# Talking-heads attention with two MLPs: half of the score sends on GpSimd's queue, two more places for copies, one query load per head pair

## Chip, cores and metric

The kernel runs on one core of a Trainium2 chip. The metric is the device time of one execution in microseconds (us), as the median of several runs. A profile belongs to one further execution, which has its own time.

## The reference

There are 4 batches, 12 heads, 448 rows and a head width of 64; all values are float32. The attention mixes the heads before and after the softmax, and two MLPs follow on 1792 tokens of width 768.

```python
scores = scale * np.matmul(q, k.transpose(0, 1, 3, 2))
scores = np.einsum('bhij,hg->bgij', scores, w_pre)        # mix of heads
attn = np.exp(scores - np.max(scores, axis=-1, keepdims=True))
attn = attn / (np.sum(attn, axis=-1, keepdims=True) + 1e-09)
attn = np.einsum('bhij,hg->bgij', attn, w_post)           # second mix
x = np.matmul(attn, v)                                    # (b, h, i, d) -> tokens x 768
...
h = x @ w_in                                              # 768 -> 2048
x = (h * np.cos(h)) @ w_out                               # 2048 -> 768
h = np.maximum(np.maximum(x @ w1, x @ w2), x @ w3)        # 768 -> 768
return h @ w_out2
```

## The kernel before, in words

**Score blocks.** Each batch's 448 rows are cut into four blocks of 10, 12, 12 and 11 "slots" of 10 rows (`SBLK`; the last overlaps the third by two rows), 16 blocks in all. Two blocks make a half of a batch. For each block and pair of heads, `qk` multiplies queries by keys on TensorE into two PSUM banks, one for each head; `evac` copies each bank to an SBUF tile s (on VectorE or ScalarE); `send` is a DMA that carries that copy to a grid tile t. The partitions of s are rows; those of t are (row within slot, head) after 4 spare partitions (`PAD`), so that the mix of heads is a matmul over partitions. There are two grids, used in turn; the 4 spare partitions of each are cleared once by `fill`, a DMA from a tile of zeros on ACT's queue.

**Visits.** A block is worked off in visits of two slots. `mix1` (L700) mixes heads from t into PSUM and needs all twelve sends of its block; `rowmax` on VectorE and `soft` on ScalarE make the exponentials e; `guard`, `recip` and `wscale` on VectorE make the divided weights w2s; `mix2` (L741) mixes the exponentials; `keep` copies the result to a2. After the two blocks of a half, `av` (L770) multiplies by the values, `keepx` copies and `out` writes to xT in DRAM. Then come the MLPs, whose first layer's weights and tokens are read and converted while the last blocks are at work.

**Loads and queues.** `qget` (queries), `kget` (keys), `vget` (values), `send`, `out` and the weights' loads are all issued on SP's queue, in one order; ACT's queue carries the first batch's keys, the small weights and `fill`. In DRAM each head's queries stand twice, one copy after the other, so that either head of a pair can be read into either half of the partitions. `qget` is two loads of 64 partitions. GpSimd issues no DMA. Each engine and queue works in the order in which its instructions were written.

**The order.** Class `Plan` deals it when the program is built. Every step has a rank, engines with a cost in us each, steps that it comes after, and places that it takes from a ring of buffers (`BUFS`: s has 6) and frees. The planner goes on in its own reckoned time; of the steps that could start on an engine it takes the one of lowest rank, and where a step may go to several engines, the one that would end first. Steps with `turn=True` are written in the order in which they were added. A copy takes a place of s, and its `send` gives it back, when it has landed.

Of the kernel before, what the change touches and what calls it, by code (L numbers as in the profile page):

```python
# [21 lines left out]
RI = 10  # L22
# [561 lines left out]
def attention(ctx, tc, q, k, v, w_pre, w_post, same_row, xT, tp, mlps):  # L584
# [12 lines left out]
    q = q.rearrange("(b c g d e i) -> b c g d e i", b=B, c=H // 2, g=2, d=2, e=D)  # L597
# [9 lines left out]
    zero = const.tile([PAD, S], F32, name="zero")  # L607
# [3 lines left out]
    for x in (zero, wraw, blk, w1):  # L611
        nc.vector.memset(x, 0.0)
# [5 lines left out]
    score = [(b, i0, RI * slots, slots) for b in range(B) for i0, slots in SBLK]  # L618
# [6 lines left out]
    def fill(n, _):  # L625
        nc.scalar.dma_start(grids[n][:PAD], zero.unsqueeze(1).to_broadcast([PAD, RT, S]))
# [47 lines left out]
    def qk(n, hp, _):  # L674
        b, i0, m, _ = score[n]
# [68 lines left out]
    def half_of(n):  # L744

        n = n // 2 * 2
        return score[n][1], score[n + 1][1] + score[n + 1][2] - score[n][1]

    def keep(v, y, eng):
        n, t, _ = visits[v]  # L750
        half = n // 2
        if ("a2", half) not in live:
            live["a2", half] = ap_.tile([128, JB, H, NHALF], F32, name="a2")
        o = (n % 2) * score[n - 1][2] + RI * (t + y)
        copy(eng, live["a2", half][:, :, :, o:o + RI].rearrange("p j g i -> p (j g) i"),
             live["a", v, y][:].rearrange("p j g a r -> p (j g) (a r)"))
# [5 lines left out]
    def av(n, x, _):  # L762
        m, a2 = score[n - 1][2] + score[n][2], live["a2", n // 2]
        for hp in pairs(x):
            vt = live["v", score[n][0], hp]
# [7 lines left out]
    def keepx(n, hp, eng):  # L773

        xs = live["xs", hp] = xp.tile([128, NHALF], F32, name="xs")
        ps = live["av", hp]
        c = 0
        for x in (n - 1, n):
            _, i0, m, slots = score[x]
            o = i0 - half_of(n)[0]  # L780
            copy(eng, xs[:, o:o + m].rearrange("p (r t) -> p r t", t=slots),
                 ps[:, c:c + m].rearrange("p (t r) -> p r t", r=RI))
            c += m

    def out(n, hp, eng):
        b, (i0, m) = score[n][0], half_of(n)
        queue_of[eng].dma_start(xT[hp * 128:(hp + 1) * 128, b * S + i0:b * S + i0 + m], live["xs", hp][:, :m])
# [10 lines left out]
    HP, per = H // 2, len(SBLK)  # L798
# [4 lines left out]
    for n in range(2):  # L803
        add(fill, (n,), -45.0 + 5.0 * n, {"A": 0.9}, lands=6.0)
    add(wmix, (0,), -39.0, {"V": 0.8}, [("wget", 0), ("wget", 2)])
    add(wmix, (1,), -39.0, {"V": 0.2}, [("wget", 1), ("wget", 2)])
    for n in range(NS):
        b = score[n][0]
        start, end = n % per == 0, n % per == per - 1
        for hp in range(HP):  # L810
            r = (first[n - 1] + 0.5 + 1.5 * hp) if n else -40.0 + hp
            if start:
                early = 8.0 if b else 20.0
                add(qget, (b, hp), r - early, {"D": 1.17}, turn=True, takes=["q"], lands=3.0)
                add(kget, (b, hp), r - early, {"D": 0.5} if b else {"A": 0.6}, turn=True, takes=["k"], lands=3.0)
# [3 lines left out]
            for h in range(2 * hp, 2 * hp + 2):  # L819
                add(evac, (n, h), r, {"A": 0.55, "V": 0.62}, [("qk", n, hp)], turn=True, takes=["s"], frees=[(ring, ("qk", n, hp), h % 2)])  # L820
                if h == 0:
                    plan.add(("new_t", n), r, lambda _: None, {}, [("evac", n, 0)], takes=["t"])
                add(send, (n, h), r, {"D": 0.83}, [("evac", n, h), ("new_t", n)], turn=True, frees=[("s", ("evac", n, h))], lands=3.0)


    for y, (n, t, slots) in enumerate(visits):
# [12 lines left out]
        for c in slots:  # L839
            begin = n % 2 == t == c == 0  # L840
# [4 lines left out]
    for n in range(1, NS, 2):  # L845
        b = score[n][0]
        last = (first + [N])[n + 1] - 1
        ends = [("keep", y, a) for y, x in enumerate(visits) if x[0] in (n - 1, n) for a in x[2]]
        start = ends[0]
        for x in range(HP // 2):  # L850
            r = last + 2.5 + 3.0 * x
            for hp in pairs(x) if n // 2 % 2 == 0 else ():
                add(vget, (b, hp), r - 10.0, {"D": 0.88}, turn=True, takes=["v"], lands=3.0)
            add(av, (n, x), r, {"T": 3.25}, [("vget", b, hp) for hp in pairs(x)] + ends, turn=True, takes=["ps_t"] * 2,
                frees=[("a2", start)] + [("v", ("vget", b, hp)) for hp in pairs(x) if n // 2 % 2])
            for hp in pairs(x):
                add(keepx, (n, hp), r, {"A": 0.45, "V": 0.5}, [("av", n, x)], turn=True, takes=["xs"], frees=[("ps_t", ("av", n, x), hp % 2)])
                add(out, (n, hp), r, {"D": 0.45}, [("keepx", n, hp)], turn=True, frees=[("xs", ("keepx", n, hp))], lands=3.0)
# [144 lines left out]
    for n in range(2):  # L1003
        r = (r0, N - 1)[n] + RANK[("fx", "x1")[n]]
        add(xget, (n,), r, {"D": 3.9}, [("out", 1, hp) for hp in range(H // 2)] + [("out", 3, hp) for hp in range(H // 2)] + [("xget", 0)] * n
# [38 lines left out]
    plan.add(("open_late",), N, open_late, {}, [("keepx", NS - 1, hp) for hp in range(HP)], behind=att_keys)  # L1044
# [70 lines left out]
    halves = 0  # L1115
    for i, (name, (eng, _, needs)) in enumerate(unit.items()):
        kind, x = name
        tags = ["wf"] if kind == "get" and x != "S3" else []
        if kind == "high":
            tags = ["w"] * (halves % 2 == 0)  # L1120
            halves += 1
# [52 lines left out]
```

## Time and profile before

| | |
|---|---|
| median of 3 runs | 1209.25 us (1206.21 to 1214.73) |
| the profiled execution | 1209.98 us |
| its span, first to last instruction | 1208.2 us |
| mean granted TensorE clock | 0.98 of full |
| TensorE (PE) busy | 1150.8 us, 95% |
| VectorE (DVE) busy | 929.1 us, 77% |
| ScalarE (ACT) busy | 637.9 us, 53% |
| GpSimd (POOL) busy | 190.3 us, 16% |
| sends, t<-s on SP's queue | 192 |

Busy shares are means over stages with different limits: the attention part lasts to some 405 us, the MLPs from there to the end. The program names its tiles in the rows: t<-s is a send, mps<-t,w the first mix, aps<-w2s,e the second, ps<-k,q (and aps or mps<-k,q for the first block) the scores, aps<-a,v the product with the values. A "q" behind an engine's name (SPq, ACTq) means what its sequencer issues, DMAs above all. "Before" is the idle time in front of an instruction and what ended it, as far as the profile can tell; where several things were waited for, it is the one that came last by the records.

### The profile page before, as it was taken

The numbers are of one execution on the slowest core, as the hardware profiler recorded it, in microseconds if no ns is written. First come the engines' busy times: TensorE is split into PE (matmuls) and PEld (weight loads), VectorE is DVE, ScalarE is ACT, GpSimd is POOL, SyncE is SP. The second block draws the span as 40 slices with busy tenths as digits, with TensorE's granted clock in tenths as the row PEclk, the third lists the DMA queues.
The fourth block names the chain that finished last, engine by engine and source line by source line (L and its number), as shares of the span: only waits on it lengthen the run. The fifth ranks groups of instructions, "written<-read, shape, count | busy, mean of one in ns | idle before, by whom it ended". The sixth has DMA issues, their size and how long they took to land.

```text
span 1208.2 us, 29520 instructions
## 1 busy us (share of the span) xinstructions
PE 1150.8 (95%) x11886; PEld 938.8 (78%) x11886; DVE 929.1 (77%) x1913; ACT 637.9 (53%) x1436; POOL 190.3 (16%) x172
## 2 busy tenths in 40 slices
PE   4879999999999889999999999999999999999998
PEld 1445655656556779999999999999998989889997
DVE  2666786788789699999999999996865548865445
ACT  1555665566568577565555555555644444344520
POOL 0000000000003120000000000001065455476340
PEclk8889999999999989999999999999999999999999
DMA  6765565654555536444444344430012221322112
GB/s 152 203 186 153 172 177 166 189 177 131 165 153 181 193 99 171 132 128 131 125 131 129 114 131 113 130 111 27 1 53 66 66 66 54 130 71 81 33 59 92
DMA packets 85384, 146.19 MB, mean 121 GB/s; under 512 B 9664, under 2 KB 68224, under 8 KB 85248
## 3 DMA queue, kind: packets, MB, share of 16 engines
q1 hardware_dynamic: 83680, 142.75, 39.8%
q10 hardware_dynamic: 1568, 1.57, 0.6%
q8 instruction: 93, 1.52, 0.5%
q14 instruction: 43, 0.35, 0.1%
HBM read 84.96 MB, written 20.45 MB: 87 GB/s over the span
## 4 chain that ended last, share of the span: by engine, by line
PE 80%; DMA 7%; DVE 6%; issue 3%; POOL 2%; ACT 1%; SPq 0%; DVEq 0%; POOLq 0%; ACTq 0%
PE ps L165 19%; PE ps L167 19%; PE ps L166 19%; PE mps L700 6%; PE aps L770 6%; PE aps L741 6%; PE ps L681 5%; DMA t<-s 3%; DVE nm L708 2%; DMA wf<-w 2%; POOL w L309 1%; DVE wf L298 1%; DMA q<-in_q_dram 1%; DVE a L600 1%; DMA wraw<-in_w_in_dram 1%
## 5 line engine op out<-in xcount | busy, mean ns | idle before, releaser
L165 PE MATMUL ps<-x,w 128*128 128x448 f32 x708 | 262.0, 370 | 6.9 <-ACT x L152 5.1
L167 PE MATMUL ps<-x,w 128*128 128x448 f32 x708 | 259.9, 368 | 1.9 <-DVE x L156 1.3
L166 PE MATMUL ps<-x,w 128*128 128x448 f32 x708 | 260.3, 368 | 0.0
L309 POOL TENSOR_TENSOR w<-wf,w 128x384 fp32r<-128x384 f32 x126 | 142.6, 1154 | 546.7 <-DVE wt L264 370.4
L165 PE MATMUL ps<-gh,w 128*128 128x448 f32 x528 | 193.8, 367 | 0.0
L166 PE MATMUL ps<-gh,w 128*128 128x448 f32 x528 | 193.5, 366 | 0.0
L167 PE MATMUL ps<-gl,w 128*128 128x448 f32 x528 | 193.3, 366 | 0.0
L714 ACT ACTIVATE e<-mps,nm 128x448 f32<-128x448 f32 (+1 forms) x184 | 117.2, 639 | 89.5 <-DVE nm L708 59.6
L165 PEld LDWEIGHTS ps<-x,w 128*128 128x128 f32 x708 | 133.5, 189 | 23.9 <-ACT x L152 5.7
L741 PEld LDWEIGHTS aps<-w2s,e 60*64 60x64 f32 x5760 | 109.1, 136 | 50.3 <-issue 22.6
L167 PEld LDWEIGHTS ps<-x,w 128*128 128x128 f32 x708 | 133.4, 188 | 15.0 <-DVE x L156 2.4
L166 PEld LDWEIGHTS ps<-x,w 128*128 128x128 f32 x708 | 133.6, 189 | 11.2 <-POOL w L132 0.2
L708 DVE TENSOR_REDUCE nm<-mps 128x1 f32<-128x448 f32 (+1 forms) x184 | 110.5, 615 | 32.1 <-PE mps L700 30.7
L700 PE MATMUL mps<-t,w 64*64 64x448 f32 (+1 forms) x720 | 108.8, 573 | 17.7 <-DMA t<-s 10.8
L741 PE MATMUL aps<-w2s,e 60*64 60x60 f32 x5760 | 113.6, 221 | 7.0 <-DVE w2s L728 3.5
L681 PE MATMUL ps<-k,q 64*64 64x448 f32 (+3 forms) x736 | 102.2, 573 | 17.3 <-ACT s L600 11.8
L298 DVE TENSOR_TENSOR wf<-wf 128x384 f32<-128x384 f32 x72 | 57.8, 815 | 71.7 <-POOL w L309 43.8
L306 ACT CAST w<-wf 128x384 fp32r<-128x384 f32 x126 | 60.6, 512 | 90.8 <-DVE wf L298 40.6
L167 PEld LDWEIGHTS ps<-gl,w 128*128 128x128 f32 x528 | 99.1, 188 | 9.0
L165 PEld LDWEIGHTS ps<-gh,w 128*128 128x128 f32 x528 | 99.1, 188 | 8.8
L166 PEld LDWEIGHTS ps<-gh,w 128*128 128x128 f32 x528 | 99.1, 188 | 8.6
L947 DVE TENSOR_TENSOR acc<-ps,acc 128x448 f32<-128x448 f32 x168 | 100.3, 613 | 3.1 <-PE ps L167 3.1
(99 smaller groups left out, 1638.6 us busy)
## 6 DMA issues: line engine op xcount, KB each, us to landing
t<-s SPq DMA_DIRECT2D x96, 210.0 KB
wf<-w SPq DMA_DIRECT2D x96, 192.0 KB
wraw<-in_w_out_dram SPq DMA_DIRECT2D x44, 384.0 KB
wraw<-in_w_dram SPq DMA_DIRECT2D x36, 384.0 KB
wraw<-in_w_in_dram SPq DMA_DIRECT2D x32, 384.0 KB
t<-s SPq DMA_DIRECT2D x48, 192.5 KB
w<-wf SPq DMA_DIRECT2D x48, 192.0 KB
t<-s SPq DMA_DIRECT2D x48, 175.0 KB
```

Source lines behind the costliest of these rows:

```text
L165: mm(w[0], x[0], start=first, stop=False)
L166: mm(w[1], x[0], start=False, stop=False)
L167: mm(w[0], x[1], start=False, stop=last)
L298: eng(raw[x], raw[l], raw[r])
L309: return nc.gpsimd.tensor_sub(A[x][1], w(), f32(A[x][0]))
L681: nc.tensor.matmul(live["s", n, 2 * hp + g][r:end], live["q", b, hp][half, i0 + r:i0 + end], live["k", b, hp][half], start=True, stop=True)
L700: nc.tensor.matmul(live["m", v, a][64 * y:64 * y + 64], w1[k], grids[n % 2][k, t + y, :], start=True, stop=True)
L708: nc.vector.tensor_reduce(nm, of(v, live["m", v, a]), axis=AX.X, op=ALU.max, negate=True)
L714: nc.scalar.activation(of(v, e), of(v, live["m", v, a]), AF.Exp, bias=live["nm", v, a], scale=1.0, accum_out=live["z", v][:, a:a + 1])
L741: nc.tensor.matmul(live["a", v, y][64 * c:64 * c + 64, j, :, a, :], live["e", v, a][k, o:o + 64], live["w2s", v][k, a], start=True, stop=True)
L770: nc.tensor.matmul(ps[64 * g:64 * g + 64, :m], vt[:, j, g, :], a2[:, j, 2 * hp + g, :m], start=j == 0, stop=j == JB - 1)
L947: return nc.vector.tensor_add(acc, po, acc) if fg else nc.scalar.copy(acc, po)
```

## The change

Sends of odd heads go to GpSimd's queue, those of even heads stay on SP's. `fill` becomes a memset on GpSimd of the 4 spare partitions of each grid; the tile of zeros goes. s has 8 places instead of 6, and in the very first block the copies of heads 1, 3, 5, 7 and 9 take the five places of e instead. `qget` becomes one load of 128 partitions: the second copy of a pair's first head and the first copy of its second head, which stand side by side in DRAM. The planner's costs and ranks follow. The table of blocks is written in another way (`HALVES`), with the functions that read it.

```diff
-SBLK = [(0, 10), (100, 12), (220, 12), (338, 11)]
+HALVES = [[[10, 12], [12, 11]]] * B
-BUFS = {"k": 10, "q": 9, "s": 6, "e": 5, "w2s": 3, "v": 7, "xs": 6, "a2": 2, "ps_m": 3, "ps_t": 3, "ps_x": 2}
+BUFS = {"k": 10, "q": 9, "s": 8, "e": 5, "w2s": 3, "v": 7, "xs": 6, "a2": 2, "ps_m": 3, "ps_t": 3, "ps_x": 2}
...
-    q = q.rearrange("(b c g d e i) -> b c g d e i", b=B, c=H // 2, g=2, d=2, e=D)
+    q = q.rearrange("(b c e i) -> b c e i", b=B, c=H // 2, e=4 * D)
...
-    zero = const.tile([PAD, S], F32, name="zero")
...
+    for b, sizes in enumerate(HALVES):
+        i = 0
+        for n, half in enumerate(sizes):
+            start, column = i, 0
+            for slots in half:
+                i = min(i, S - RI * slots)
+                score.append((b, i, RI * slots, slots, 2 * b + n, column))
+                column += RI * slots
+                i += RI * slots
+            halves.append((b, start, i - start, column, range(len(score) - len(half), len(score))))
...
     def fill(n, _):
-        nc.scalar.dma_start(grids[n][:PAD], zero.unsqueeze(1).to_broadcast([PAD, RT, S]))
+        nc.gpsimd.memset(grids[n][:PAD], 0.0)
...
-        for g in range(2):
-            queue_of[eng].dma_start(live["q", b, hp][64 * g:64 * g + 64], q[b, hp, g, 0])
+        queue_of[eng].dma_start(live["q", b, hp], q[b, hp, D:3 * D])
...
+    def copy_place(n, h):
+        return ("e", ep) if n == 0 and h in range(1, 2 * BUFS["e"], 2) else ("s", sp)
+
     def evac(n, h, eng):
         m, ps = score[n][2], live["s", n, h]
-        s = live["s", n, h] = sp.tile([128, S], F32, name="s")
+        place, pool = copy_place(n, h)
+        s = live["s", n, h] = pool.tile([128, S], F32, name=place)
         copy(eng, s[:m], ps[:m])
 
-    def send(n, h, _):
+    def send(n, h, eng):
         slots = score[n][3]
-        nc.sync.dma_start(grids[n % 2][PAD + h:PAD + RI * H:H, :slots, :], live.pop(("s", n, h))[:RI * slots])
+        queue_of[eng].dma_start(grids[n % 2][PAD + h:PAD + RI * H:H, :slots, :], live.pop(("s", n, h))[:RI * slots])
...
-        add(fill, (n,), -45.0 + 5.0 * n, {"A": 0.9}, lands=6.0)
+        add(fill, (n,), -60.0, {"P": 5.0})
...
-            r = (first[n - 1] + 0.5 + 1.5 * hp) if n else -40.0 + hp
+            r = (first[n - 1] + 0.5 + 0.125 * score[n - 1][3] * hp) if n else -40.0 + hp
...
-                add(qget, (b, hp), r - early, {"D": 1.17}, turn=True, takes=["q"], lands=3.0)
+                add(qget, (b, hp), r - early, {"D": 0.57}, turn=True, takes=["q"], lands=3.0)
...
-                add(send, (n, h), r, {"D": 0.83}, [("evac", n, h), ("new_t", n)], turn=True, frees=[("s", ("evac", n, h))], lands=3.0)
+                add(send, (n, h), r, ({"D": 0.83}, {"P": 0.55})[h % 2], [("evac", n, h), ("new_t", n)], turn=True, frees=[(place, ("evac", n, h))], lands=3.0)
...
-                add(out, (n, hp), r, {"D": 0.45}, [("keepx", n, hp)], turn=True, frees=[("xs", ("keepx", n, hp))], lands=3.0)
+                add(out, (half, hp), r, {"D": 0.5}, [("keepx", half, hp)], turn=True, frees=[("xs", ("keepx", half, hp))], lands=3.0)
```

## Rows read from the trace of the kernel before

**Rows 1.** Windows: start:end, length, busy us (instructions) by engine, clock, DMA share, GB/s.

```profile
core 0: us, PE busy (x) PEld busy (x) DVE busy (x) ACT busy (x) POOL busy (x), PEclk, DMA share, GB/s
0.00:30.00 30.00, 13.06 (x57) 3.50 (x58) 8.28 (x22) 4.99 (x9) 0.20 (x4) 0.82 0.61 151
30.00:60.00 30.00, 24.47 (x456) 12.14 (x454) 18.02 (x46) 15.07 (x40) 0.00 (x0) 0.84 0.71 204
60.00:90.00 30.00, 23.02 (x571) 13.52 (x566) 18.88 (x51) 16.23 (x43) 0.00 (x0) 0.83 0.70 186
90.00:120.00 30.00, 28.11 (x631) 17.52 (x631) 19.73 (x56) 14.97 (x45) 0.00 (x0) 0.94 0.53 153
120.00:180.00 60.00, 57.08 (x1412) 35.68 (x1404) 48.55 (x126) 37.18 (x103) 0.00 (x0) 1.00 0.58 173
...
480.00:540.00 60.00, 60.00 (x296) 55.34 (x295) 58.86 (x121) 34.56 (x67) 0.00 (x0) 1.00 0.44 127
```

**Rows 2.** The page: granted TensorE clock in 40 slices of the span, in tenths.

```profile
PEclk8889999999999989999999999999999999999999
```

**Rows 3.** Timeline of the opening: start us, us, engine, line, operation, tiles, [idle before].

```profile
0.73 12.49 SPq L660 DMA_DIRECT2D q<-in_q_dram  x12
...
7.87 1.15 DVE L600 COPY s<-ps 100x448 f32<-100x448 f32 x2 [2.63 <-PE ps L681]
...
13.34 18.74 SPq L691 DMA_DIRECT2D t<-s  x14
...
13.37 1.46 ACTq L626 DMA_DIRECT2D t<-zero  x2
...
14.69 1.69 PE L681 MATMUL mps<-k,q 64*64 64x448 f32 x8
...
23.18 1.28 ACT L600 ACT_TABLE_LOAD   x1 [23.18 <-DMA t<-s]
...
32.45 0.62 DVE L600 COPY s<-ps 120x448 f32<-120x448 f32 x1 [16.53 <-DMA t<-s]
...
34.53 1.84 PE L700 MATMUL mps<-t,w 64*64 64x448 f32 x8
```

**Rows 4.** Chain that ended last, 0 to 130 us: start us, us, what.

```profile
13.34 9.75 DMA t<-s
...
25.11 3.91 DMA t<-s
...
67.15 8.19 DMA t<-s
...
75.41 3.14 DMA t<-s
```

**Rows 5.** Timeline at the changes to blocks 1 and 2.

```profile
49.39 1.65 SPq L691 DMA_DIRECT2D t<-s  x2
...
53.71 1.77 PE L700 MATMUL mps<-t,w 64*64 64x448 f32 x8 [3.06 <-DMA q<-in_q_dram]
...
78.68 1.77 PE L700 MATMUL mps<-t,w 64*64 64x448 f32 x8 [6.13 <-DMA t<-s]
```

**Rows 6.** TensorE's waits, 125 to 200 and 200 to 360: sum us, times, longest.

```profile
PE mps L700 <- DMA t<-s: 3.4, 2, 2.2
...
PE mps L700 <- DMA t<-s: 1.3, 1, 1.3
```

**Rows 7.** Windows of almost only sends, and of loads alone; columns as above.

```profile
24.00:33.00 9.00, 4.84 (x17) 1.16 (x17) 0.55 (x1) 5.19 (x10) 0.00 (x0) 0.50 0.58 187
1.00:10.00 9.00, 4.84 (x16) 1.14 (x16) 5.32 (x14) 0.00 (x0) 0.00 (x0) 1.00 0.97 234
```

**Rows 8.** Views of single tiles and lines: ns min/median/max, first and last start us.

```profile
L691 SPq DMA_DIRECT2D t<-s x192: 755/756/3322, 13.3 to 358.4; - x192
...
L660 SPq DMA_DIRECT2D q<-in_q_dram x48: 465/546/1312, 0.7 to 266.9; - x48
...
L615 DVE MEMSET v<- x7: 485/485/485, 1.5 to 4.8; 128x512 f32 x7
...
L132 POOL TENSOR_TENSOR w<-wf,w x30: 999/1022/1402, 369.9 to 1169.5; 128x384 fp32r<-128x384 f32 x30
```

**Rows 9.** Groups by line: busy us, mean ns, idle before.

```profile
L728 DVE TENSOR_TENSOR w2s<-w2t,rz 128x120 f32<-128x120 f32 (+1 forms) x92 | 26.4, 287 | 0.8
```

More of the change, by code (lines that the diff above doesn't have):

```diff
@@ L615, in attention @@
         nc.vector.memset(x, 0.0)
-    score = [(b, i0, RI * slots, slots) for b in range(B) for i0, slots in SBLK]
+    score, halves = [], []
+    for b, sizes in enumerate(HALVES):
[8 more added lines that the diff above has]
+            halves.append((b, start, i - start, column, range(len(score) - len(half), len(score))))
     visits = [(n, t, range(min(2, x[3] - t))) for n, x in enumerate(score) for t in range(0, x[3], 2)]
@@ L674, in qk @@
     def qk(n, hp, _):
-        b, i0, m, _ = score[n]
+        b, i0, m = score[n][:3]
         for g in range(2):
@@ L760, in pairs, with av @@
         return 2 * x, 2 * x + 1
-    def av(n, x, _):
-        m, a2 = score[n - 1][2] + score[n][2], live["a2", n // 2]
+    def av(half, x, _):
+        b, _, _, m, _ = halves[half]
+        a2 = live["a2", half]
         for hp in pairs(x):
-            vt = live["v", score[n][0], hp]
+            vt = live["v", b, hp]
             live["av", hp] = ps_t.tile([128, JB, H, RI], F32, name="aps")
@@ L771, in av, with keepx, out @@
                                      start=j == 0, stop=j == JB - 1)
-    def keepx(n, hp, eng):
+    def keepx(half, hp, eng):
         xs = live["xs", hp] = xp.tile([128, NHALF], F32, name="xs")
         ps = live["av", hp]
[L777 to L780, printed above, removed]
+        for n in halves[half][4]:
+            _, i0, m, slots, _, c = score[n]
+            o = i0 - halves[half][1]
             copy(eng, xs[:, o:o + m].rearrange("p (r t) -> p r t", t=slots),
                  ps[:, c:c + m].rearrange("p (t r) -> p r t", r=RI))
-            c += m
-    def out(n, hp, eng):
-        b, (i0, m) = score[n][0], half_of(n)
+    def out(half, hp, eng):
+        b, i0, m = halves[half][:3]
         queue_of[eng].dma_start(xT[hp * 128:(hp + 1) * 128, b * S + i0:b * S + i0 + m], live["xs", hp][:, :m])
@@ L796, in add @@
             before[f] = [key]
-    HP, per = H // 2, len(SBLK)
+    HP = H // 2
     for x in range(3):
@@ L808, in attention @@
         b = score[n][0]
-        start, end = n % per == 0, n % per == per - 1
+        start, end = score[n - 1][0] != b or not n, n == NS - 1 or score[n + 1][0] != b
         for hp in range(HP):
-            r = (first[n - 1] + 0.5 + 1.5 * hp) if n else -40.0 + hp
+            r = (first[n - 1] + 0.5 + 0.125 * score[n - 1][3] * hp) if n else -40.0 + hp
             if start:
                 early = 8.0 if b else 20.0
-                add(qget, (b, hp), r - early, {"D": 1.17}, turn=True, takes=["q"], lands=3.0)
+                add(qget, (b, hp), r - early, {"D": 0.57}, turn=True, takes=["q"], lands=3.0)
                 add(kget, (b, hp), r - early, {"D": 0.5} if b else {"A": 0.6}, turn=True, takes=["k"], lands=3.0)
@@ L839, in attention @@
         for c in slots:
-            begin = n % 2 == t == c == 0
+            begin = n == halves[score[n][4]][4][0] and t == c == 0
             add(keep, (y, c), i + 1.5, {"A": 0.57, "V": 0.65}, [key("mix2")], turn=True, takes=["a2"] * begin,
                 frees=[("ps_t", key("mix2"), c)])
[L845 to L848, printed above, removed]
+    for half, (b, _, _, _, members) in enumerate(halves):
+        last = (first + [N])[members[-1] + 1] - 1
+        ends = [("keep", y, a) for y, x in enumerate(visits) if x[0] in members for a in x[2]]
         start = ends[0]
@@ L851, in attention @@
             r = last + 2.5 + 3.0 * x
[L852 removed]
+            for hp in pairs(x) if half % 2 == 0 else ():
                 add(vget, (b, hp), r - 10.0, {"D": 0.88}, turn=True, takes=["v"], lands=3.0)
[L854 to L855 removed]
+            add(av, (half, x), r, {"T": 3.25}, [("vget", b, hp) for hp in pairs(x)] + ends, turn=True, takes=["ps_t"] * 2,
+                frees=[("a2", start)] + [("v", ("vget", b, hp)) for hp in pairs(x) if half % 2])
             for hp in pairs(x):
[L857 to L858 removed]
+                add(keepx, (half, hp), r, {"A": 0.45, "V": 0.5}, [("av", half, x)], turn=True, takes=["xs"], frees=[("ps_t", ("av", half, x), hp % 2)])
+                add(out, (half, hp), r, {"D": 0.5}, [("keepx", half, hp)], turn=True, frees=[("xs", ("keepx", half, hp))], lands=3.0)
     FG = mlps.GROUPS
@@ L1043, in attention @@
     first_layer(0)
-    plan.add(("open_late",), N, open_late, {}, [("keepx", NS - 1, hp) for hp in range(HP)], behind=att_keys)
+    plan.add(("open_late",), N, open_late, {}, [("keepx", len(halves) - 1, hp) for hp in range(HP)], behind=att_keys)
     for r, job in sorted(jobs):
```

18 lines of the change are left out of this document (7 added, 11 removed).

## Prediction, made before the changed kernel was run

> **What bounds the kernel now.** I first read busy time by stretch [rows 1], to see where TensorE is short of work. From 480 us on it shows none: 60.00 of 60 us are busy in the second half's stretches, so what the attention part ends earlier, the kernel ends earlier. In the steady attention part TensorE is busy 57.08 of 60 us. The holes lie in the first 120 us: 30 - 13.06 = 16.9 us, then 5.5, 7.0 and 1.9 us, 31 us in all. In the first 90 us the granted clock is also below full, 0.82 to 0.84, a mixture of its two levels, 1.2 and 2.4 GHz [rows 1, 2].
>
> Next I read the timeline of the opening, engine by engine, to see what comes last there [rows 3]. SP spends 12.49 us on twelve query loads and only then, at 13.34 us, starts the sends (the copies of scores that go to the grid t). The first copies on VectorE began at 7.87 us. TensorE has all products of score block 0 at 14.69 + 1.69 = 16.4 us. Then copying stops: ScalarE's first copy is held until 23.18 us and VectorE's next until 32.45 us (16.53 us idle), both by a send's landing. With six places for copies, the seventh copy waits until the first send has landed, 9.75 us after its issue [rows 4]. The first mix of heads (L700) starts at 34.53 us. So the opening is bound by places, then by the landing of sends, then by SP.
>
> Last come the chain of waits and TensorE's own stalls at the changes of score block: the chain runs through sends of 8.19 and 3.14 us before block 2 [rows 4], and TensorE sits 3.06 us before block 1 and 6.13 us before block 2 [rows 5]. The first is put down to a query load, but the last two sends of block 1 are issued just before it, at 49.39 to 51.04 us [rows 5], so I read it as a send. Later such waits are few: 3.4 us in 125 to 200 us, 1.3 us in 200 to 360 us [rows 6].
>
> **The change, part by part.** *Block layout.* The new table gives the same starts and lengths (0, 100, 220, 338 with 10, 12, 12, 11 slots; halves of 220 and 228 rows): no cost, no gain.
>
> *Query loads.* Twelve loads per batch become six of double size. The bytes stay. At a median of 546 ns [rows 8] 24 x 0.55 = 13 us leave SP over the run. In the opening SP may be held by the transfers: 1 to 10 us has DMA busy 0.97 at 234 GB/s [rows 7], so data arrive little earlier, but SP is free for the first send about when the first copy is done, at 9 to 11 us instead of 13.3.
>
> *Places.* Block 0 gets 7 places of s and 5 of e: all twelve copies can be made with no landing awaited. The e tiles are next written by the exponentials of block 0, which come after all its sends anyway, so this adds no wait. VectorE makes a pair's two copies in 1.15 us [rows 3], so the last pair's are done about 16.4 + 1.2 = 17.6 us.
>
> *Spare partitions.* Two DMAs of the zeros leave ACT's queue (1.46 us of issue [rows 3]) and one clearing leaves VectorE; no send is then in flight beside them. Two memsets of 4 x 5376 elements go to GpSimd, ahead of its first send. No such instruction is in the trace. Bounds: VectorE clears 512 elements a partition in 485 ns [rows 8], which makes 5.1 us for one and 10.2 us for two; GpSimd's two-input subtract takes 1.02 us for 384 [rows 8], which makes 14.3 and 28.6 us. I take the first, since it is the same operation with one write and no read. GpSimd is then free at about 11 us.
>
> *Sends.* 96 of 192 sends move from SP to GpSimd. On SP one takes 756 ns [rows 8], so 73 us leave SP, and odd heads no longer stand behind loads of queries, keys and values on its queue. GpSimd issues no DMA in this trace. Bounds of one: 0.76 us (as on SP) to 1.4 us (the longest L132 subtract on GpSimd, its nearest kind of work [rows 8]); I take 0.9, six in 5.4 us. Nothing else stands on GpSimd until the MLP's weight steps, whose opening waits for the last send in any case, so it is GpSimd's waits for copies that the odd sends queue behind, and no other engine's work.
>
> **The opening's sum.** Last copy 17.6, issue to 18.4, landing 3.91 [rows 4]: 22.3 us. By bytes: 12 x 175 KB = 2.1 MB at the 187 GB/s of a stretch with almost only sends [rows 7] is 11.2 us from 10 to 11 us on: 22 us. I take 24, for loads still in flight. Against 34.5 us that is **-10 us**. Ends: 22 gives -12.5; the slow memset puts GpSimd's sends at 29 to 33.6 and their landing at 37.5, which gives +3.
>
> **Block changes, 45 to 105 us.** The stalls before blocks 1 and 2 and the hole of 90 to 120 us are 3.1 + 6.1 + 1.9 = 11.1 us [rows 1, 5]. They come from sends queued behind loads on one queue and from six places; eight places and a second queue remove part. The bytes remain and so does a DMA that is over half busy, hence I take about half, **-5 us** (ends 0 and -11.1). *Later blocks:* 4.7 us of waits [rows 6], take **-2 us** (0 to -4.7). *Clock:* 24.47 + 23.02 = 47.5 us of TensorE work in 30 to 90 us ran at 0.835 [rows 1]; at full speed it would be 39.7, so up to -7.8 us; the trace has the clock at 0.50 in 24 to 33 us [rows 7], when TensorE waits most, and I take **-1 us**. *Order:* the planner sees other costs and deals the order of work anew; I take 0, with 4 us either way, the size of the 3 us hole in a steady 60 us stretch [rows 1].
>
> Sum: -10 - 5 - 2 - 1 = -18 us. The profiled execution took 1209.98 us (span 1208.2 and 1.8 around it), so 1192.0; the median of the runs is 0.73 lower, which makes 1191.3. What is late next is TensorE itself, 95% busy in steady attention.
>
> A rule that bears on the bytes: in 24 to 33 us, with almost only sends, DMA is busy 0.58 of sixteen engines, while loads reach 0.97 [rows 7]. The Trainium skill (DMA: Bandwidth & Descriptors, section "Why a DMA increments its semaphore by 16 and not by 1") says that a transfer is spread over the largest number up to 16 that divides both sides' first dimension, which is 10 for these sends, always the lowest on SP's queue, but from a moving start on GpSimd's. By it the low ten engines would carry 0.5 + 0.5 x 10/16 = 0.81 of the send bytes, an estimate: 2.1 us less for each 11.2 us, some 6 us over the three early blocks instead of 5.
>
> **The rivals.** *Only the opening gains.* The early block changes may be bound by what DMA moves: 204 GB/s in 30 to 60 us at 0.71 busy [rows 1]. The change moves the same bytes, so the stalls stay and later sends come early in vain. For it: sends land in 8.19 us there, over twice the 3.91 us of a quieter stretch [rows 4]. Against it: VectorE and ScalarE are seen waiting for places. Opening -10, rest +1: 1200 (1196 to 1205).
>
> *GpSimd's sends land late.* Every block's first mix needs all twelve sends. If an odd send lands x us after its even neighbour would have, each of the fifteen later changes of block may pay x: 15x - 10. It gains nothing from x = 0.7 on and loses over 1% from x = 1.5; at x = 2 it is +20: 1229. For it: after 125 us there are still waits for sends [rows 6], so the cover is thin in places. Against it: a difference of 0.15 to 0.65 us in issue, by the bounds above, and only six sends on the queue for each block.
>
> *VectorE starves GpSimd.* VectorE is busy 48.55 of 60 us in steady attention [rows 1]. If a GpSimd send went on only in the remaining 19%, 0.76 us would become 4.0 us and six of them 24 us, over the (358.4 - 13.3)/16 = 21.6 us of a block [rows 8]: +2.4 x 16 = +38: 1247. The only row on it speaks against: GpSimd's subtract runs in 1.02 us at the median, 1.4 at most, the attention part included [rows 8]; and most of VectorE's work there reads PSUM, its scaling of w2s, the largest between SBUF tiles, being 26.4 us in the whole run [rows 9]. The Trainium skill (SBUF — State Buffer, section "SBUF: two separate sides") has this rule: descriptors of a GpSimd DMA can't be written while VectorE runs in a two-port mode. No run here shows a GpSimd DMA yet.
>
> *It doesn't do what it says:* if the first sends stand behind slow memsets, the opening is +3 and the rest -8: 1205. This is the far end of the first term.
>
> **How the numbers follow.** Forecast (1180 to 1198 its own spread) 0.57; only the opening, with the slow memsets, 0.26; late landing 0.13; starved 0.04. The predicted time is the likeliest case's, 1191. The sum of the favourable ends (-12.5 - 11.1 - 4.7 - 7.8 - 4 = -40) won't come together; two of its larger ones do at about 1180. The high end takes in the second case, the slow memset with the order's 4 us (1209) and the mild part of late landing (x = 1, +5): 1214. Some 0.06 lies below and 0.12 above. A change under 1% (12 us) can't well be told from none here. Faster by over 1%, under 1197: nearly all of the forecast and a small part of the second case, 0.58. Slower by over 1%, over 1221: most of late landing and all of starving, 0.13. Between: 0.29.
>
> **What would show it.** The first L700 matmul at 22 to 26 us instead of 34.5 (opening); no copy waiting on a send before it (places); two memsets on GpSimd ending at 10 to 12 us (a longer one refutes the price); 96 sends on GpSimd's queue at 0.76 to 1.4 us; TensorE busy over 27 of 30 us in 30 to 60 and 60 to 90 us, with stalls before blocks 1 and 2 under 3 us each; waits for t<-s after 125 us under 5 us in sum; the second half's stretches unchanged, only earlier. The prediction is wrong if TensorE waits at each block for odd sends, if early blocks stay at 25 us with DMA as busy as before, or if the time won by 120 us is lost again before 440 us.

## The result, and the profile after

The changed kernel is slower: 1223.58 us median (1218.46 to 1227.03, 7 runs) against 1207.94 us (1202.49 to 1214.73, 7 runs), a ratio of 1.0122, 95% interval [1.0089, 1.0155]. The forecast was 1191 in 1180 to 1214. The profiled execution took 1220.23 us with a span of 1218.4. Its windows, with the columns of [rows 1]:

```profile
0.00:30.00 30.00, 13.36 (x65) 3.14 (x66) 9.24 (x23) 4.80 (x9) 13.39 (x13) 0.75 0.76 224
30.00:60.00 30.00, 23.41 (x380) 11.90 (x381) 16.16 (x40) 13.71 (x36) 4.75 (x9) 0.74 0.77 178
60.00:90.00 30.00, 24.35 (x655) 16.07 (x649) 21.07 (x56) 18.00 (x50) 4.78 (x9) 0.89 0.73 187
90.00:120.00 30.00, 29.50 (x721) 18.43 (x720) 23.70 (x65) 17.55 (x52) 3.90 (x7) 1.00 0.46 126
120.00:180.00 60.00, 56.00 (x1374) 34.81 (x1374) 46.58 (x124) 34.22 (x95) 9.24 (x16) 1.00 0.61 169
480.00:540.00 60.00, 60.00 (x297) 55.38 (x296) 58.79 (x121) 37.88 (x76) 0.00 (x0) 1.00 0.48 138
```

Against [rows 1] the first 60 us hold no more TensorE work than before (36.8 us against 37.5), 60 to 120 us hold 2.7 us more, and steady attention 1.1 us less in 60. From 30 to 60 us DMA is busier (0.77 against 0.71) and moves less (178 GB/s against 204). The starts of the blocks, read off each block's first mix, tell where the time goes: block 0 starts at 34.5 us in both kernels, block 4 at 122.7 (127.2 before), block 8 at 214.0 (217.3), block 15 at 371.8 (364.2), and the last mix ends at 395.2 (386.1). So 4.5 us are won by 123 us and 13.6 lost from there to the last mix. What follows it is as long as before (823 and 822 us).

The timeline of the opening and of two later places, with the columns of [rows 3]:

```profile
0.76 9.08 POOL L635 MEMSET t<- 4x5376 f32 x2 [0.29 <-POOLq L1169]
0.76 4.81 SPq L668 DMA_DIRECT2D q<-in_q_dram  x6
...
7.31 7.79 SPq L674 DMA_DIRECT2D v<-in_v_dram  x6
...
9.79 2.98 POOL L703 DMA_DIRECT2D t<-e  x5
...
17.04 0.56 ACT L600 COPY s<-mps 100x448 f32<-100x448 f32 x1
18.40 0.90 SPq L703 DMA_DIRECT2D t<-s  x1
...
19.35 2.67 SPq L674 DMA_DIRECT2D v<-in_v_dram  x6
...
22.55 7.89 SPq L703 DMA_DIRECT2D t<-s  x7
...
34.48 2.02 PE L712 MATMUL mps<-t,w 64*64 64x448 f32 x8
...
55.63 1.77 PE L712 MATMUL mps<-t,w 64*64 64x448 f32 x8 [4.92 <-DMA t<-s]
...
83.01 0.37 PE L753 MATMUL aps<-w2s,e 60*64 60x60 f32 x3 [5.08 <-issue]
```

GpSimd does what the forecast wanted: both memsets end at 9.84 us, five sends follow at once, and all copies of block 0 are made by 17.6 us. SP does not: the shorter query loads leave room on it, and the planner gives that room to loads of values (L674), ahead of the even heads' sends. These start at 18.40 us instead of 13.34 [rows 3]; the last 3.2 us before it SP waits for a value load. Hence the same first mix, L712 after as L700 before. The waits for sends that answer to [rows 6] are 0.5 us in 125 to 200 and 5.5 us in 200 to 360 (3.4 and 1.3 before):

```profile
PE mps L712 <- DMA t<-s: 0.5, 1, 0.5
PE mps L712 <- DMA t<-s: 5.5, 3, 3.3
```

### The profile page after: what moved, and what is told of

Same layout as the page of the kernel before. It is cut to its first block, busy times and chain, and to the rows that moved or that the text cites. A ratio compares the mean times of both kernels' runs of the same rounds, so it can differ in the third digit from the quotient of the medians.

```text
span 1218.4 us, 29564 instructions
## 1 busy us (share of the span) xinstructions
PE 1150.9 (94%) x11886; PEld 940.4 (77%) x11886; DVE 937.4 (77%) x1918; ACT 637.6 (52%) x1429; POOL 254.2 (21%) x271
## 4 chain that ended last, share of the span: by engine, by line
PE 74%; DVE 8%; DMA 7%; issue 6%; ACT 2%; POOL 2%; SPq 0%; ACTq 0%; DVEq 0%; POOLq 0%
PE ps L165 19%; PE ps L167 19%; PE ps L166 19%; PE mps L712 5%; PE aps L753 5%; PE aps L777 5%; PE ps L689 4%; DMA t<-s 3%; DVE wf L298 1%; DMA wf<-w 1%; DMA wraw<-in_w_in_dram 1%; DVE x L445 1%; DVE nm L720 1%; DMA q<-in_q_dram 1%; POOL w L309 1%
## 5 line engine op out<-in xcount | busy, mean ns | idle before, releaser
L309 POOL TENSOR_TENSOR w<-wf,w 128x384 fp32r<-128x384 f32 x126 | 139.6, 1131 | 549.4 <-DVE wt L264 370.4
L165 PEld LDWEIGHTS ps<-x,w 128*128 128x128 f32 x708 | 133.8, 189 | 26.3 <-ACT x L152 7.8
L167 PEld LDWEIGHTS ps<-x,w 128*128 128x128 f32 x708 | 133.6, 189 | 16.3 <-DVE x L156 2.2
L712 PE MATMUL mps<-t,w 64*64 64x448 f32 (+1 forms) x720 | 109.3, 580 | 17.6 <-DMA t<-s 11.0
L689 PE MATMUL ps<-k,q 64*64 64x448 f32 (+3 forms) x736 | 107.6, 587 | 18.4 <-ACT s L600 12.5
L703 POOL DMA_DIRECT2D t<-s x91 | 53.2, 584 | 301.1 <-DVE s L600 116.0
```

The source lines that it names most:

```text
L165: mm(w[0], x[0], start=first, stop=False)
L167: mm(w[0], x[1], start=False, stop=last)
L309: return nc.gpsimd.tensor_sub(A[x][1], w(), f32(A[x][0]))
L712: nc.tensor.matmul(live["m", v, a][64 * y:64 * y + 64], w1[k], grids[n % 2][k, t + y, :], start=True, stop=True)
```

## The experiments

Two theories stood at first: **late sends** (what GpSimd sends lands later, or costs more DMA time, whatever the order) and **new order** (the planner, seeing other costs, deals a worse order). A third, **places**, came up on the way. Each ratio is to the kernel before, run beside it.

**1. GpSimd's sends in the order of before, and SP's sends in the order of after.**

```
pool_old_order (on before; the planner still reckons with SP):
- nc.sync.dma_start(grids[n % 2][...], live.pop(("s", n, h))[...])
+ (nc.gpsimd if h % 2 else nc.sync).dma_start(grids[n % 2][...], ...)
sp_new_order (on after; the planner still reckons with GpSimd):
- queue_of[eng].dma_start(grids[n % 2][...], ...)
+ nc.sync.dma_start(grids[n % 2][...], ...)
before_new_rank (on before):
- r = (first[n - 1] + 0.5 + 1.5 * hp) if n else -40.0 + hp
+ r = (first[n - 1] + 0.5 + 0.125 * score[n - 1][3] * hp) if n else -40.0 + hp
```

> The kernel before with one change: odd heads' sends are issued by GpSimd, while the planner still reckons them on SP, so that the order on TensorE, VectorE and ScalarE is that of before to the instruction. If GpSimd's sends as such are the cause (they land late), this is slower than before by about what the changed kernel is, 8 to 16 us. If the newly dealt order is the cause, it is not slower: between -8 us and +2 us against before.

> The changed kernel with one thing put back: all sends are issued by SP, while the planner still reckons odd ones on GpSimd, so that the order on TensorE, VectorE and ScalarE is that of the changed kernel. If late GpSimd sends are the cause, it comes back to within 4 us of before (1204 to 1212 us). If the newly dealt order is the cause, it stays slow, 1218 us or more, and SP's fuller queue may add some.

> The kernel before with one line of the planner changed: the rank of a block's score products takes the slots of the block before (0.125 a slot and pair) instead of 1.5 a pair, as in the changed kernel. Nothing that runs is different but the order. If the order alone is worth several us either way, this differs from before by over 4 us (no sign foretold); if order is of no weight, it is within 3 us.

Measured: 1.0122 [1.0056, 1.0189], 1.0001 [0.9977, 1.0025] and 1.0007 [0.998, 1.0033]. Moving half of the sends to GpSimd costs 1.2%, some 15 us, in the old order as in the new one. The new ranks alone do nothing. But "late sends" is not the whole: `sp_new_order` has the clearing, the places and the query loads of the change and gains nothing by them, and experiment 5 will show 17 us lost there by its order. The windows from block 4's first mix to the last mix, in the kernel before, `pool_in_turn` (experiment 3: order of before, 96 sends on GpSimd), the changed kernel and `sp_new_order`, show the same:

```profile
127.20:386.10 258.90, 248.94 (x5964) 152.87 (x5964) 206.40 (x536) 160.14 (x444) 9.03 (x8) 0.99 0.55 166
```

```profile
129.20:395.60 266.40, 250.91 (x5964) 153.25 (x5965) 206.54 (x535) 160.16 (x442) 46.51 (x73) 0.99 0.59 160
```

```profile
122.70:395.20 272.50, 252.90 (x5967) 156.72 (x5967) 209.42 (x540) 160.82 (x439) 46.63 (x73) 0.98 0.57 157
```

```profile
111.00:386.00 275.00, 252.92 (x5967) 157.47 (x5967) 210.23 (x542) 161.84 (x441) 9.10 (x8) 0.98 0.53 156
```

Of the 13.6 us that the changed kernel loses here, 7.5 are there with GpSimd's sends in the old order, and 6 more come with the rest of the change. With that and every send on SP the stretch is no shorter, so it is not the queue alone. Each is one execution, which can lie 5 us from its kernel's median.

**2. How many sends, and which second queue.** `pool_all` sends all heads from GpSimd, `pool_first4` the odd heads of the first four blocks (24 sends), `pool_not_last` heads 1, 3, 5 and 7 (64 sends); `act_old_order` sends the odd heads from ACT's queue. All are on the kernel before, in its order; each edit is the first diff with another condition or queue.

> The kernel before with all 192 sends on GpSimd, all orders kept. Theory 'each GpSimd transfer costs DMA time': about twice the loss of 96, +20 to +32 us, and DMA busy time up by some 12% after 125 us. Rival 'two queues of sends disturb each other': sends are on one queue again, beside SP's loads only, so the loss is smaller than with 96, under +10 us.

> The kernel before with odd heads' sends on GpSimd in blocks 0 to 3 alone (24 of 192), all orders kept. If the loss lies where DMA is fullest, the first 125 us, most of the +15 us is here: +8 us or more. If every block pays about alike (the profile's division: 3.4 of 10.7 us before block 4), it is +2 to +6 us.

> The kernel before with odd heads' sends on ACT's queue, all orders kept. Theory 'GpSimd's transfers themselves load the DMA engines more': ACT's are like SP's, so DMA busy time for the same bytes stays within 3% of before, sends land as before (3.6 to 5.7 us), and only ScalarE's issue time is lost (96 x 0.75 us = 72 us on an engine that is about 60% busy there), 0 to +8 us. Rival 'two queues of sends disturb each other, whichever engine issues': DMA busy time rises as with GpSimd (by 6% after 125 us, 12% before), landings grow by 0.6 us or more, and the time is +12 us or more.

> The kernel before with the sends of heads 1, 3, 5 and 7 on GpSimd (64 of 192), heads 9 and 11 back on SP, all orders kept. If the loss is that the last odd send of each block lands late, it falls below +4 us. If GpSimd's transfers load the DMA engines and make all land later, it stays near the +15 us of 96 sends: +8 us or more.

Measured: 1.0126 [1.0075, 1.0177], 1.0024 [1.0001, 1.0047], 1.0061 [1.003, 1.0091], 1.0299 [1.0246, 1.0352]. So 192 sends cost what 96 cost, which fits neither range; the price does not grow with the number of sends. (In the trace of `pool_all` 6.3 us of it lie in the opening, whose first mix comes at 40.8 us.) Four blocks with GpSimd sends cost some 2.9 us together, in an interval that begins at nothing; that fits a price for each block and a price for each send alike. And 64 sends cost more than twice as much as 96, which neither theory had. The view of waits (34 to 372 us: sum, times, longest) of the kernel before and of `pool_not_last` shows where that went:

```profile
DVE s L600 <- DMA t<-s: 4.1, 2, 2.1
```

```profile
DVE s L600 <- DMA t<-s: 45.4, 10, 17.7
```

The longest, 17.7 us, is the opening's and ends at 35.0 us; the like wait of before (16.53 us, [rows 3]) ends at 32.45 and so lies outside the window. That leaves 27.7 us against 4.1. VectorE, about to copy scores, waits for a place. The built programs say why. With all sends on one queue the tile pool hands out its six places strictly in turn: each comes round after 6 copies. With two queues among the senders it does not: after 3 to 9 copies in `pool_old_order`, 1 to 9 in `pool_not_last`, 5 to 11 of eight places in the changed kernel. In `pool_not_last` head 3's copy often gets the place of head 1, two copies back, and stands until that send has landed. That is the third theory, and a fault in the reading of experiment 1: `pool_old_order` differed from before in its places too.

**3. Places in turn, and out of turn without GpSimd.** `pool_in_turn`, `not_last_in_turn` and `after_in_turn` are `pool_old_order`, `pool_not_last` and the changed kernel with named tiles (`copied_to`) in turn; `sp_out_of_turn` is the kernel before with every send on SP and, nearly, the places of `pool_not_last` (`ORDER` is a list of 192 numbers). In that one, one copy of the 192 is overwritten before it is sent, so that one head of one block is mixed from another's scores; its instructions and their order are those of before.

```
- s = live["s", n, h] = sp.tile([128, S], F32, name="s")
+ s = live["s", n, h] = next_place()
in next_place():
+ return copied_to[copies % len(copied_to)]
in next_place() of sp_out_of_turn:
+ return copied_to[int(ORDER[copies])]
```

> The kernel before with the odd heads' sends on GpSimd, every engine's order as before, as in the earlier run of that edit (1.012), but the six places of copies are handed out strictly in turn. In that earlier run the places came round after 3 to 9 copies instead of always 6, and VectorE's copies waited 8.9 us for places from 34 to 400 us, against 4.1 us in the kernel before. Theory 'sends land late': the cost is in GpSimd's transfers, so it stays, 1.009 to 1.014, 1215 to 1222 us. Rival 'places out of turn': it goes, 0.998 to 1.004, 1203 to 1211 us.

> The kernel before with heads 1, 3, 5 and 7 sent by GpSimd (64 sends), places handed out in turn. Without that it was 1.030: there a place came round after 1 to 9 copies, and VectorE's copies waited 45.4 us for places. 'Places out of turn': all of what it lost over the run with 96 sends goes, and the rest too, 0.998 to 1.004. 'Sends land late': what is above 1.012 goes, the rest stays: 1.006 to 1.013, 1211 to 1222 us.

> The kernel before with all sends on SP and every order as before; the six places are given to the copies in the list in which the run with heads 1, 3, 5 and 7 on GpSimd had them. The places alone, without GpSimd. If out-of-turn places made that run's 1.030, this one is 1.015 to 1.035, 1222 to 1247 us, with VectorE's copies waiting 20 to 50 us for places. If GpSimd's transfers made it, 0.997 to 1.005, 1202 to 1211 us.

> The changed kernel with its eight places for copies handed out strictly in turn (they came round after 5 to 11 copies). Its copies waited only 0.4 us on VectorE and 0.6 us on ScalarE for places, so 'sends land late' has it unchanged: 1.008 to 1.015, 1216 to 1226 us. 'Places out of turn' has it fall towards the version without GpSimd's sends: 0.985 to 0.998, 1190 to 1206 us.

Measured: 1.0144 [1.0086, 1.0203], 1.0102 [1.0068, 1.0137], 1.0301 [1.0268, 1.0333], 1.0151 [1.0107, 1.0194]. The same row of waits in `sp_out_of_turn`, and then in `not_last_in_turn`:

```profile
DVE s L600 <- DMA t<-s: 35.1, 11, 5.6
```

```profile
DVE s L600 <- DMA t<-s: 1.6, 2, 1.0
```

Both causes are real and now apart. Places out of turn make 3% by themselves, without one send from GpSimd, and account for what 64 sends cost above 96. The two do not add: with such places the 64 sends on GpSimd cost nothing more (1.0299 and 1.0301). Places are not the cause in the changed kernel: with its eight places put in turn it is as slow as it was. What stays in the old order with GpSimd sends in all blocks, 1.0 to 1.4%, is the sends.

**4. The sends by themselves.** A kernel with no attention, the probe: single sends, then bursts of twelve, each ended by a copy on VectorE that waits for the last to land.

> No attention and no MLP at all, the output is zeros: only sends of the kernel's shape (120 rows of 448 into 10 partitions), each set ended by a small VectorE copy that needs all of them. Five single sends on SP, GpSimd and ACT in turn, then bursts of twelve, as of one block: all on SP, half on GpSimd, all on GpSimd, half on ACT; three of each, then the same behind four key loads on SP. Theory 'a GpSimd send lands late': a single one takes 0.5 to 1.1 us longer from issue to the copy than SP's. Theory 'GpSimd's transfers load the DMA engines more': bursts with GpSimd take longer than SP's (which is 12 x 0.76 us of issue and the last landing, some 12 us) in spite of the second queue, by 1 us or more. If neither, bursts of half and half end 2 to 5 us sooner than SP's.

One execution, 479.03 us. Its timeline; the bracket on a copy is the wait for the send or the burst. In order: a single send from SP, GpSimd and ACT; two bursts from SP; two from SP and GpSimd in turn; two from GpSimd; two from SP and ACT:

```profile
19.19 0.19 DVE L71 COPY mark<-t 124x64 f32<-124x64 f32 x1 [3.28 <-DMA t<-s]
...
37.34 0.19 DVE L71 COPY mark<-t 124x64 f32<-124x64 f32 x1 [3.53 <-DMA t<-s]
...
55.72 0.20 DVE L71 COPY mark<-t 124x64 f32<-124x64 f32 x1 [3.33 <-DMA t<-s]
...
80.53 0.19 DVE L71 COPY mark<-t 124x64 f32<-124x64 f32 x1 [14.05 <-DMA t<-s]
94.98 0.20 DVE L71 COPY mark<-t 124x64 f32<-124x64 f32 x1 [14.26 <-DMA t<-s]
...
126.45 0.20 DVE L71 COPY mark<-t 124x64 f32<-124x64 f32 x1 [16.89 <-DMA t<-s]
143.11 0.19 DVE L71 COPY mark<-t 124x64 f32<-124x64 f32 x1 [16.46 <-DMA t<-s]
...
174.90 0.20 DVE L71 COPY mark<-t 124x64 f32<-124x64 f32 x1 [15.93 <-DMA t<-s]
191.43 0.19 DVE L71 COPY mark<-t 124x64 f32<-124x64 f32 x1 [16.34 <-DMA t<-s]
...
221.12 0.20 DVE L71 COPY mark<-t 124x64 f32<-124x64 f32 x1 [13.75 <-DMA t<-s]
236.34 0.20 DVE L71 COPY mark<-t 124x64 f32<-124x64 f32 x1 [15.03 <-DMA t<-s]
```

A single GpSimd send is 0.25 us later (median of five), less than expected. A burst of twelve takes 14.2 us from SP (mean of three), 16.3 us mixed and 15.9 us from GpSimd alone: 2.1 and 1.8 us more, though GpSimd issues in 0.58 us what takes SP 0.76. SP and ACT took 13.75 and 15.03 us; their third burst, 16.45, ran beside the key loads of the next set. The queues' rows (packets, MB, share of 16 engines' time) say what grows, first 66.5 to 109.5 us with SP's bursts, then 109.5 to 158.5 with the mixed ones, then 158.5 to 207 with GpSimd's:

```profile
q1 hardware_dynamic: 4680, 7.74, 52.1%
...
q0 software_dynamic: 1440, 3.88, 36.4%
q1 hardware_dynamic: 2340, 3.87, 29.4%
...
q0 software_dynamic: 2880, 7.75, 72.1%
```

The share times 16 and the window's length is DMA engine time: 358 us for 7.74 MB from SP, 46 us per MB. Mixed, GpSimd's half costs 285 us for 3.88 MB, 74 per MB, and SP's half beside it 60; GpSimd alone 72. In the two undisturbed bursts of SP and ACT both halves cost 45 to 47, so it is not a second queue as such. The same bytes take half as much DMA time again. GpSimd's data packets are of three rows (5376 bytes) where SP's are of one (1792). Behind four key loads on SP the medians of three bursts are 15.5 (SP), 17.1 (mixed), 16.8 (GpSimd) and 16.6 us (SP and ACT), with single bursts from 15.0 to 25.0; there ACT's are no better than GpSimd's.

The kernel shows the same. Windows of the kernel before, and of `pool_in_turn`, which differs by the queue of 96 sends alone, with the columns of [rows 1]:

```profile
35.00:125.00 90.00, 76.29 (x1793) 45.88 (x1788) 60.67 (x160) 49.63 (x134) 0.00 (x0) 0.90 0.64 177
125.00:245.00 120.00, 114.73 (x2698) 70.08 (x2692) 92.77 (x243) 70.77 (x198) 0.00 (x0) 0.99 0.59 177
```

```profile
35.00:125.00 90.00, 75.76 (x1733) 46.64 (x1727) 59.27 (x158) 47.81 (x131) 12.81 (x22) 0.88 0.75 173
125.00:245.00 120.00, 111.25 (x2552) 67.57 (x2552) 88.49 (x232) 68.00 (x189) 18.04 (x31) 0.97 0.63 168
```

DMA share per GB/s rises by 20% (0.64/177 to 0.75/173) in the first stretch and by 13% in the second, and TensorE loses 3.5 us in the second. Loads pay as well: key loads on SP land after 8.0 us, against 5.1, at the median of the six between 120 and 240 us.

**5. What the rest of the change is worth.** `all_but_pool` is the changed kernel with every send on SP and reckoned there; `all_but_pool_held` also holds the loads of values and of the second batch behind block 0's last send; `held_six_places` is that with six places for copies, none of them of e; `after_loads_held` has the changed kernel's GpSimd sends and the held loads.

```
all_but_pool:     - add(send, (n, h), r, ({"D": 0.83}, {"P": 0.55})[h % 2], ...)
                  + add(send, (n, h), r, {"D": 0.83}, ...)
loads held, too:  - add(vget, (b, hp), r - 10.0, {"D": 0.88}, ...)
                  + add(vget, (b, hp), r - 10.0, {"D": 0.88}, [("send", 0, 11)] * (b == 0), ...)
```

> The changed kernel, with the first batch's values and the second batch's queries and keys held back in the planner until the last send of block 0 is dealt. If the opening's gain was lost because those loads went ahead of the even heads' sends, the first L-mix matmul comes at 23 to 27 us instead of 34.5, and some of the 8 to 11 us stays to the end: 1210 to 1218 us. If the sends' own landing sets the opening, it stays at 33 us or more and the time at 1220 or more.

> The change without its GpSimd sends: places, memset, one query load, new ranks; all sends on SP and reckoned there; the loads that went ahead in the opening held back behind block 0's sends. If the opening's gain is real and the newly dealt order is not worse later, 8 to 16 us faster than before (1189 to 1197 us). If the later blocks give it back as they did with the changed kernel's order on SP, within 3 us of before.

> The change without its GpSimd sends, all sends on SP and reckoned there, and the loads not held back: three pairs of value loads go ahead of block 0's sends. Against the run with loads held back (0.9905 of before) it shows what the loads ahead cost. If the opening's gain hung on them, the first mix comes at 28 to 33 us and the time is 3 to 8 us above that run (1197 to 1202 us at its level of before).

> The fast version (no GpSimd sends, loads held back) with six places for copies again and none of e. If the places made the opening, the first mix is back at 30 us or more and most of the 12 us gain is lost (0.996 to 1.002 of before). If the memsets and the query loads made it, the first mix stays by 26 us and the ratio at 0.99 to 0.995.

Measured: 1.0106 [1.0069, 1.0142] with the first mix at 27.5 us; 0.9905 [0.9875, 0.9935] at 24.0; 0.9858 [0.9824, 0.9892] at 26.3; 0.9901 [0.9867, 0.9935] at 25.0. The fastest is `all_but_pool`, 1187.32 us, 17 us under the kernel before. Holding the loads was expected to help `all_but_pool` and did not. An early first mix is not enough: with GpSimd's sends and the order dealt for them, 7 us won in the opening are gone by block 15 (370.6 us, against 364.2 before). Eight places and e's are worth nothing here. `all_but_pool` and `sp_new_order` differ only in whether the planner reckons odd sends on SP or on GpSimd; both send from SP, and they lie 1.4%, 17 us, apart (0.9858 and 1.0001). So the order dealt for two queues, run from SP, costs as much as the sends do. Their windows from block 4 to the last mix say where: 257.4 and 275.0 us, with TensorE idle for 9.4 and 22.1.

**6. Which edit brings it.** `sp_fill_by_load` clears the spare partitions by two loads on ACT's queue as before (seven places), `sp_two_query_loads` splits each query load again; both on `all_but_pool`.

```
- nc.gpsimd.memset(grids[n][:PAD], 0.0)
+ nc.scalar.dma_start(grids[n][:PAD], zero.unsqueeze(1).to_broadcast([PAD, RT, S]))

- queue_of[eng].dma_start(live["q", b, hp], q[b, hp, D:3 * D])
+ for g in range(2):
+     queue_of[eng].dma_start(live["q", b, hp][64 * g:64 * g + 64], q[b, hp, D + D * g:2 * D + D * g])
```

> The fastest version so far (the changed kernel with every send on SP and reckoned there; 0.986, first mix at 26.3 us) with the spare partitions cleared again by two loads on ACT's queue instead of GpSimd, and seven places for copies (the cleared constant takes the room of the eighth). If the opening gained because those loads and the copies that waited for ScalarE's queue went away, as the forecast has it, it is slower by 2 to 6 us, 0.988 to 0.992, with the first mix at 28 to 31 us. If the query loads made the opening, it stays: 0.983 to 0.988, first mix at 25 to 28 us.

> The same fastest version with a pair's queries loaded in two halves again (12 issues on SP instead of 6 in the opening, 48 instead of 24 in all), reckoned at 1.17 us. If the query loads made the opening, the first mix goes back by the six issues and their transfers to 29 to 33 us and the time to 0.990 to 0.997, 1194 to 1202 us. If the clearing made it, the first mix stays at 25 to 28 us and the time at 0.983 to 0.989.

Measured: 0.9945 [0.9923, 0.9968] and 0.9926 [0.99, 0.9952]. Both edits carry part, 0.9 and 0.7% of 1.4%, each give or take 0.4. The opening is the clearing's. Timelines of `all_but_pool` and of `sp_fill_by_load`:

```profile
12.68 0.90 SPq L703 DMA_DIRECT2D t<-s  x1
13.68 0.76 SPq L703 DMA_DIRECT2D t<-e  x1
14.54 0.76 SPq L703 DMA_DIRECT2D t<-s  x1
...
26.33 1.77 PE L712 MATMUL mps<-t,w 64*64 64x448 f32 x8 [0.32 <-DMA t<-s]
```

```profile
13.69 1.49 ACTq L636 DMA_DIRECT2D t<-zero  x2
14.27 0.76 SPq L704 DMA_DIRECT2D t<-e  x1
15.12 3.04 SPq L704 DMA_DIRECT2D t<-s  x1
...
18.27 3.14 SPq L704 DMA_DIRECT2D t<-e  x1
...
21.51 2.41 SPq L704 DMA_DIRECT2D t<-s  x1
...
33.17 0.98 PE L713 MATMUL mps<-t,w 64*64 64x448 f32 x1
```

While the two clearing loads are in flight (their packets go on to 23.7 us), three sends on SP take 2.4 to 3.1 us to issue instead of 0.76, and the first mix comes at 33.2 us. With two query loads a pair it comes at 27.3 us; that edit's 0.7% is spread over the blocks.

## Why the prediction was wrong

**Two steps failed,** "Sends" and "Order". The forecast was -18 us and the kernel came out at +15; the sends are some 15 us of that gap and the order some 17.

**"Sends"** priced the 96 moved sends by their issue alone (0.9 us each, and "73 us leave SP") and let the transfer stand as it was. The issue was dearer on paper than on the chip: 0.58 us. The transfer was not as before: a block's burst lands 2.1 us later in the probe, and 96 sends cost 15 us in the old order (experiment 1), which would be 1.0 us for each of 15 changes of block. The rival "GpSimd's sends land late" had the mechanism and the form, so much for each block, and its reason against, issue times 0.15 to 0.65 us apart and only six sends on the queue, was the error: it compared issues, not landings under load. It had 13%. That its formula, 15x - 10, meets the measured 14.7 us at x = 1.6 is chance: the opening's -10 us did not come, and the order, which it leaves out, added its part.

**"Order: I take 0, with 4 us either way"** took its margin from a hole in the steady stretch, not from a newly dealt order. The order dealt for two queues cost 17 us with every send on SP (experiment 5). Where GpSimd does send, the stretch from block 4 on is 6 us longer than in the old order (experiment 1). The prediction's own sign came true: the time won by 120 us was lost again before 440. Which of the planner's choices makes that order worse stays open.

**The opening's sum**, 24 us, holds as a sum of what must happen: 24.0 us in `all_but_pool_held`, though with all sends on SP. In the changed kernel it was 34.5, since "Order" failed there too: SP was reckoned free of half of its sends and filled with value loads. The same order with SP's sends has 31.0, so 3.5 us of it are GpSimd's. Holding the loads gave 7 us of the opening back and 2 us of the time, no more than the runs can tell from nothing.

**What bounds the kernel now.** The opening was said to be bound by places first. The copy that VectorE held until 32.45 us has 120 rows, so it is one of block 1 and not in the way of the first mix; only ScalarE's of 23.18 us was. Nor were places the limit: six do as well as eight and five of e (0.9901 and 0.9905). The late landings made the copies wait for places, and it was above all the clearing loads that made the landings late (experiment 6).

**Spare partitions.** The price was right (5.1 us estimated, 4.57 measured; GpSimd free at 9.8, forecast 11); the slow memset is refuted. That "two DMAs of the zeros leave ACT's queue" was the largest part of the opening's gain (33.2 us with them, 26.3 without); the sum gave it no term of its own.

**The whole without GpSimd's sends.** The forecast's sum was -18 us; the version with sends on SP is -17. Its parts do not match one by one, so the sum is partly luck: by the starts of the blocks the opening gains 8.2 us, the stretch to block 4 another 10.6 and the rest 1.5, where the forecast had 10, 5 and 2, and 1 for the clock. Between it and the changed kernel lie 2.7%. Of that 1.2% is the queue (1.0001 to 1.0122, same order) and 1.4% lies between an order dealt for one queue and one dealt for two, both run from SP. An order dealt for one queue, with this change's other edits and GpSimd's sends, was not run.

**VectorE starves GpSimd** is refuted in the form it was given: 91 sends from s take 574 to 603 ns each to issue, not 4 us. The Trainium skill's rule on the lock (SBUF — State Buffer, section "SBUF: two separate sides") speaks of two-port modes; no run here shows such a wait.

**The rule on the spread of engines** promised, by the prediction's estimate, 2.1 us less for each burst; the probe measured 2.1 us more. What the same page of the Trainium skill says elsewhere fits better (DMA: Bandwidth & Descriptors, section "Issuing engines are not separate DMA queues"): issuing from several engines saves only the time of issue, since the transfers share the DMA engines. The runs agree and go further: here it also costs.

**Open:** why GpSimd's three-row packets take more engine time in a burst (alone, five sends take 20.7% of 18 us from SP and 19.9% of 19 us from GpSimd, the same), and how much of the 15 us is landing, how much the loads beside it, and how much TensorE's pauses (below); and what in the order dealt for two queues costs its 17 us.

## What to carry to other kernels

Price a DMA moved to another queue by when its whole burst lands and by engine time per byte, not by its issue; a small kernel of nothing but such bursts tells it before the change is built. When users of a ring of buffers are spread over two queues, look up which buffer each step then gets: a pool that no longer goes in turn cost 3% with nothing else changed. A queue that a planner takes to be free gets filled with other work, and the order that it deals for one more queue can cost as much as the queue: run the new order on the old queues before calling it neutral.

## Of the hardware, not expected

TensorE pauses in which the trace shows no release, as the 5.08 us above, end shortly after a packet of an instruction queue. In the 19 traces of kernels with attention, all 32 such pauses of over 0.8 us between 34 and 372 us end 1.26 to 1.66 us after a 16 KB packet of queue q8 has ended (the packets come 5.8 us apart on average). Pauses before a first mix, where TensorE's sequencer had waited for a send, are not counted. The 32 sum to 0 to 3.0 us a kernel where SP does all sends, 3.8 to 9.4 us in the kernels with 96 or 192 sends on GpSimd, 4.5 in `pool_first4` and 3.4 with ACT's; with 64 they are 7.4 in `not_last_in_turn`, but 0 in `pool_not_last`. The Trainium skill (Runtime: NRT & Kernel Launch, section "Instruction fetch mechanics") has engines refilled in 16 KB blocks through a queue of their own, mostly hidden. That such a fetch, late under a busy DMA, makes the pauses was not tested by an experiment.

Sends from ACT's queue cost 0.6% too (experiment 2), though two undisturbed bursts of SP and ACT took 13.75 and 15.03 us, against 14.05 to 14.26 from SP. Why was not run.
